# Two-port rules in the list scheduler of a fused attention and FFT-mixing MLP kernel, its weight conversion moved between engines, and spare buffers for the first chunks

## Chip, cores and metric

One NeuronCore of a Trainium2 chip runs the whole kernel. The metric is device time in microseconds (us) of one execution; the table below gives three runs of the kernel before and one execution recorded by the hardware profiler.

## The reference, cut to what matters

Eight batches of 8 heads, 576 positions and head dimension 64 pass a landmark (Nyström) attention with 32 landmarks and six Newton steps; its output goes through a two-dimensional FFT, a layer norm and an MLP of width 2048. Everything is float32.

```python
q_lm = q.reshape(B, H, 32, 18, D).mean(axis=3); k_lm = ...
A, Bm, C = sm(q, k_lm), sm(q_lm, k_lm), sm(q_lm, k)
Z = Bm.T / (norm1(Bm) * norminf(Bm) + 1e-6)
for _ in range(6): Z = 2 * Z - Z @ Bm @ Z
x = (A @ Z @ C @ v) as (batch, 576, 512)
u = x + real(fft2(x))
un = (u - mean(u)) / sqrt(var(u) + 1e-6)
return u + relu(un @ w_ch1) @ w_ch2
```

## The kernel before

A float32 product is made of three float16 matmuls: each operand is split into a high half and a low half (`mm3`). **Attention** of a batch (`attention`, `landmarks`, `mix`, lines 598 to 957) is a long chain of small steps that goes to and fro between TensorE and VectorE; it ends in `norm` (line 959), which writes normalized tiles of 128 rows and has them transposed by SyncE's DMA queue into `unT`. Batch 0 gives tiles 0 to 3, batch 1 tiles 4 to 8, batch 2 from tile 9 on. **Chunks** are pairs of tiles: 18 of them go through the MLP. Chunks 0 to 4 (`chunk`, line 998) make 8 hidden blocks each: 24 matmuls into a PSUM bank `hp`, a ReLU and a split into an SBUF tile, 12 matmuls into `acc`. Chunks 5 to 17 (`seven`, line 1065) do the second product with seven half products in place of eight, for which sums of blocks of the second weight are made once (`sums_of` and `block`, lines 1036 to 1063, 24 blocks that go to DRAM and back) and differences in place.

**Weights** (`weights`, line 521). Both weights arrive as 64-bit words in 16 tiles each (`w0`, the first weight, and `w1`, the second; profiles call both `w`). A tile takes: a shift of the low word, on GpSimd for all 32 tiles (table `XP`, line 89); two VectorE operations that put sign and exponent in; one ScalarE operation; a Gram matmul that finds a power-of-two scale; a scaling into the buffer `ws`, on ScalarE for the first weight and on VectorE for the second; a ScalarE copy that makes the high half; and a subtraction that makes the low half, on GpSimd for all 16 tiles of the first weight and for 8 of the second, on VectorE for the other 8 (table `LP`).

**Order.** No instruction is placed by hand. Every operation is recorded with an estimated cost (`cost_of`), a phase and a rank. `solve` (line 226) then simulates the engines with a list scheduler and emits each engine's queue in the order found. Attention of batch b has phase 100·b, weights 40 to 70, chunk work and sums 1000 and -1. Buffers come from pools with fixed counts (`SLOTS`, line 85); pools in `IN_ORDER` hand out their slots strictly in the order of the program. On the chip nothing but semaphores between producers and consumers holds the queues to the simulated times. All operations are issued from one line, so profile rows read L1149 and are told apart by tile names.

Of the kernel before, what the change touches and what calls it, by code (L numbers as in the profile page):

```python
# [11 lines left out]
F16 = mybir.dt.float16  # L12
# [74 lines left out]
LINK, PATIENCE = 0.05, 0.0  # L87
SEVEN, RING, LATE = 5, 10, 2
XP, LP = ((1, 1, 1, 1), (1, 1, 1, 1)), ((1, 1, 1, 1), (1, 0, 1, 0))

# [77 lines left out]
class Op:  # L168
    __slots__ = ("engine", "calls", "held", "took", "phase", "group", "margin", "seq", "before", "after", "tiles", "claims", "rank", "start", "end", "nbytes", "waits", "name")


class Order:


    def __init__(self):
        self.ops, self.phase, self.group, self.margin, self.bundle, self.claims = [], 0, 0, 0.0, None, []

# [8 lines left out]

    def op(self, engine, held, took, writes, reads, call, nbytes=0):
        o = self.bundle if engine == "PE" and self.bundle else None
        if o is None:
            o = Op()  # L190
            o.engine, o.calls, o.held, o.took, o.seq = engine, [], 0.0, 0.0, len(self.ops)
            o.phase, o.group, o.margin, o.nbytes = self.phase, self.group, self.margin, nbytes
            o.before, o.after, o.tiles, o.claims, o.name = {}, [], {}, self.claims, ""
# [32 lines left out]
    def solve(self):  # L226
# [10 lines left out]
        free = dict.fromkeys(engines, 0.0)  # L237
        pipe, now, done = 0.0, 0.0, []
        self.done = done
# [26 lines left out]
        while events:  # L266
            now = events[0][0]
            while events and events[0][0] <= now + 1e-9:
                _, _, what, o = heapq.heappop(events)
                if what == "ready":  # L270
                    soon[o.engine].pop(o, None)
                    heapq.heappush(ready[o.engine], ((o.phase, -o.rank if o.group >= 0 else 0.0, o.seq), o))
                elif what == "end":
                    for t in o.tiles:
                        if not t.pool.kept:
                            t.left -= 1
                            if not t.left:
                                t.pool.free.append(t.slot)
            for e in engines:
                if free[e] > now + 1e-9 or not ready[e]:  # L280
                    continue
                found = min((x for x in ready[e] if fits(x[1])), default=None, key=lambda x: x[0])
                if found is None or any(
# [17 lines left out]
                push(free[e], "free", o)  # L301
                push(o.end, "end", o)
# [12 lines left out]
class Engine:  # L315
# [5 lines left out]
    def __getattr__(self, name):  # L321
        def emit(out, *args, **kw):
            seen = [x for x in (*args, *kw.values()) if isinstance(x, View)]
            writes = [out] + ([kw["accum_out"]] if "accum_out" in kw else [])
            reads = [x for x in seen if x is not kw.get("accum_out")]
            held, took = self.cost(name, out, reads, (*args, *kw.items()))
            self.order.op(self.name, held, took, writes, reads, (self.engine, name, (out, *args), kw))
            self.order.ops[-1].name = name

        return emit  # L330


def cost_of(engine):
# [3 lines left out]
    def cost(name, out, reads, rest):  # L337
        n = max(width(v) for v in (out, *reads))
        pointers = sum(width(v) == 1 and width(out) > 1 for v in reads)
        psum = any(v.at_psum() for v in (out, *reads))  # L340
        if engine == "DVE":
            rate = 1.04e-3
            if name in ("tensor_scalar", "tensor_copy") and not psum:
                rate = 0.82e-3 if out.dtype == I32 else 0.6e-3
            elif out.dtype == I32:
                rate = 1.45e-3 if any(v.ap.ap[-1][0] > 1 for v in reads) else 1.2e-3
            elif name == "tensor_tensor" and not psum:
                rate = 1.4e-3
            if name == "reciprocal":
                rate = 6e-3  # L350
            return 0.07 + rate * n + 0.06 * pointers, 0.08
        if engine == "ACT":
            extra = 0.1 if any(isinstance(x, tuple) and x[0] == "accum_out" for x in rest) else 0.0
            return 0.09 + 0.79e-3 * n + (0.12 if pointers else 0.0) + extra, 0.1
        if name == "memset":
            return 0.1 + 1e-3 * n, 0.1
        power = 0.6 if any(x is ALU.pow for x in rest) else 0.0
        return 0.15 + (1.5e-3 if name == "tensor_scalar" else 2.1e-3) * n + power, 0.05

# [3 lines left out]
class Kernel:  # L363
# [157 lines left out]
    def weights(self):  # L521
# [437 lines left out]
    def norm(self, b, uts):  # L959
# [23 lines left out]
        for j, ut in enumerate(uts):  # L983
# [14 lines left out]
    def chunk(self, ch):  # L998
# [126 lines left out]
    def run(self):  # L1125
# [3 lines left out]
        for b in range(self.NB):  # L1129
            self.attention(b)  # L1130
            if b == 0:
                self.weights()
            while TCH * (chunks + 1) <= self.ntile:
                (self.seven if chunks >= SEVEN else self.chunk)(chunks)
                chunks += 1
                if chunks == SEVEN - 1:
                    for i in range(NF // 2):
                        self.sums_of(i)
                elif chunks == SEVEN:
                    for i in range(NF // 2):  # L1140
                        self.differences_of(i)
# [75 lines left out]
```

## Time and profile before

| what | us |
|---|---|
| runs of the kernel before | 1063.86, 1070.26, 1071.0 (median 1070.26) |
| the profiled execution, its own time | 1063.53 |
| span of that execution, first to last instruction | 1061.7 |
| TensorE busy in the span | 963.6 |
| VectorE busy | 780.1 |
| ScalarE busy | 466.3 |
| GpSimd busy | 420.5 |

The time of the profiled execution is 1.8 us more than its span. Busy times are unions over the span, so an engine's idle time is the span less its busy time. PE is TensorE's matmul stream, DVE VectorE, ACT ScalarE, POOL GpSimd, SPq SyncE's queue of DMAs.

### The profile page before, as it was taken

Reading aid. Unit: us, or ns where it says so; the run is one execution under the profiler, and the core shown is the slowest. Engines: PE = TensorE matmul, PEld = TensorE weight load, DVE = VectorE, ACT = ScalarE, POOL = GpSimd, SP = SyncE. Lnnn points to the kernel's source line nnn. Section 1 sums busy time; section 2 is a strip of 40 time slices with the busy share of each in tenths; the row PEclk is TensorE's granted clock in tenths of the full one; section 3 lists DMA queues with packets and bytes.
Section 4 is the critical chain, followed back from the end, with each engine's and each line's share of the span. In section 5 each row is a group of like instructions: output and inputs, shape, how many; then the busy total and the mean of one; then the engine's idle time right before and its main releaser. Section 6 shows DMA issues by size and latency. Waiting matters only on the chain.

```text
span 1061.7 us, 24997 instructions
## 1 busy us (share of the span) xinstructions
PE 963.6 (91%) x9858; PEld 758.3 (71%) x9858; DVE 780.1 (73%) x2015; ACT 466.3 (44%) x997; POOL 420.5 (40%) x383
## 2 busy tenths in 40 slices
PE   4565788989899999998999899998999999999997
PEld 3344645656576666886878787787878878888886
DVE  6998888997886865648877898587977646564343
ACT  4567453443453433434443554344543343343332
POOL 2358455357432145425133514343334422332332
PEclk9576879989999999999999999999999999999999
DMA  9565402414433310245333443335334312334331
GB/s 343 183 218 165 135 1 57 162 41 88 170 95 119 70 34 1 77 114 170 101 105 77 139 142 104 89 108 161 115 89 119 116 60 71 117 105 105 114 92 49
DMA packets 139398, 117.29 MB, mean 110 GB/s; under 512 B 66704, under 2 KB 128144, under 8 KB 139152
## 3 DMA queue, kind: packets, MB, share of 16 engines
q1 hardware_dynamic: 139280, 115.69, 36.1%
q8 instruction: 77, 1.26, 0.5%
q14 instruction: 41, 0.34, 0.1%
HBM read 88.91 MB, written 12.58 MB: 96 GB/s over the span
## 4 chain that ended last, share of the span: by engine, by line
PE 39%; DVE 28%; issue 15%; POOL 8%; ACT 5%; DMA 4%; SPq 1%; POOLq 0%; DVEq 0%; ACTq 0%
PE hp L1149 15%; PE at L1149 14%; PE acc L1149 10%; DVE sum L1149 5%; POOL h L1149 5%; DVE u L1149 3%; DVE w L1149 3%; DVE row L1149 2%; DVE mt L1149 2%; DVE h L1149 1%; DVE ws L1149 1%; ACT h L1149 1%; SPq L1149 1%; DVE Wx L1149 1%; ACT ws L1149 1%
## 5 line engine op out<-in xcount | busy, mean ns | idle before, releaser
L1149 PE MATMUL hp<-unT,w 128*128 128x256 f16 x3456 | 408.3, 274 | 1.4 <-ACT ws L1149 1.4
L1149 PEld LDWEIGHTS <-w 128*128 128x128 f16 (+1 forms) x3584 | 346.9, 99 | 74.0 <-DVE w L1149 20.7
L1149 PEld LDWEIGHTS <-h 128*128 128x128 f16 x2616 | 248.7, 98 | 85.0 <-issue 9.2
L1149 POOL TENSOR_TENSOR h<-sum,h 128x640 f16<-128x640 f32 x104 | 148.7, 1432 | 329.3 <-ACT h L1149 304.1
L1149 PE MATMUL acc<-w,h 128*128 128x256 f16 (+1 forms) x1680 | 270.0, 300 | 5.7 <-DVE h L1149 2.4
L1149 DVE TENSOR_TENSOR sum<-ws 128x256 f32<-128x256 f32 (+1 forms) x312 | 141.9, 506 | 133.7 <-ACT ws L1149 126.9
L1149 ACT CAST h<-sum 128x640 f16<-128x640 f32 x104 | 75.4, 725 | 109.6 <-DVE sum L1149 108.4
L1149 PE MATMUL at<-big,h 128*128 128x256 f16 x936 | 123.0, 274 | 0.0
L1149 ACT ACTIVATE ws<-hp 128x512 f32<-128x512 f32 x104 | 61.9, 595 | 136.4 <-PE hp L1149 135.7
L1149 POOL TENSOR_TENSOR w<-ws,w 128x512 f16<-128x512 f32 (+1 forms) x40 | 45.1, 1142 | 37.6 <-ACT w L1149 36.0
L1149 POOL TENSOR_TENSOR row<-row,row 128x512 f16<-128x512 f32 x36 | 45.7, 1280 | 32.7 <-ACT row L1149 31.9
L1149 PEld LDWEIGHTS <-mt 128*128 128x128 f16 x432 | 38.9, 101 | 22.1 <-issue 14.3
L1149 PEld LDWEIGHTS <-big 128*128 128x128 f16 (+1 forms) x768 | 39.7, 103 | 15.0 <-issue 9.6
L1149 DVE TENSOR_REDUCE lm<-big 128x32 f32<-128x576 f32 (+1 forms) x48 | 44.3, 942 | 4.2 <-DMA big<-k_dram 3.3
L1149 DVE TENSOR_TENSOR h<-ws,h 128x256 f16<-128x256 f32 x104 | 47.2, 454 | 0.0
L1149 POOL TENSOR_TENSOR mt<-mt,asum 128x512 f32<-128x512 f32 x14 | 15.3, 1110 | 74.6 <-DVE asum L1149 54.2
L1149 POOL TENSOR_TENSOR ws<-ws 128x256 f16<-128x256 f32 (+1 forms) x44 | 33.8, 774 | 27.8 <-ACT ws L1149 26.6
L1149 DVE SCALAR_TENSOR_TENSOR u<-at,scw,row 128x128 f32<-128x128 f32 (+3 forms) x120 | 39.5, 386 | 5.2 <-PE at L1149 4.3
L1149 ACT CAST h<-ws 128x256 f16<-128x256 f32 x104 | 42.1, 405 | 2.6
L1149 DVE SCALAR_TENSOR_TENSOR u<-acc,winv,u 128x512 f32<-128x512 f32 (+1 forms) x62 | 37.5, 631 | 7.0 <-PE acc L1149 6.8
L1149 ACT CAST row<-row 128x512 f16<-128x512 f32 x36 | 21.7, 615 | 45.9 <-DVE row L1149 40.6
L1149 ACT ACTIVATE h<-hp 128x512 f16<-128x512 f32 x36 | 21.5, 596 | 37.6 <-PE hp L1149 37.4
(181 smaller groups left out, 1312.4 us busy)
## 6 DMA issues: line engine op xcount, KB each, us to landing
big<-sums SPq DMA_DIRECT2D x312, 128.0 KB, 2.1
w<-w_dram SPq DMA_DIRECT2D x22, 512.0 KB, 7.3
big<-v_dram SPq DMA_DIRECT2D x16, 640.0 KB, 4.4
big<-q_dram SPq DMA_DIRECT2D x16, 584.0 KB, 6.4
big<-k_dram SPq DMA_DIRECT2D x16, 576.0 KB, 5.9
out_dram<-u SPq DMA_DIRECT2D x36, 256.0 KB, 2.2
big<-w_dram SPq DMA_DIRECT2D x10, 512.0 KB, 9.5
sums<-ws SPq DMA_DIRECT2D x24, 128.0 KB, 1.7
```

The source lines that it names most:

```text
L1149: getattr(engine, name)(*map(real, args), **{k: real(x) for k, x in kw.items()})
```

## The change

The scheduler gets a flag `port` on operations: on VectorE for those with no PSUM operand that read two full SBUF operands, or are a plain copy or `tensor_scalar`, of over 4 elements; on GpSimd for all but memsets. While one flagged operation runs in the simulation (and 0.05 us after it), no other flagged one starts. Costs in `cost_of` are set anew. The shifts of all 32 weight tiles go to ScalarE, all low halves to VectorE, and every second scaling of the second weight from VectorE to ScalarE. The third `unT` comes out of the pool `big`, and every third hidden block of chunks 0 to 4 (but the first four blocks of chunk 0) out of `sum`. The sums of blocks get batch 1's last operation as a predecessor.

```diff
-XP, LP = ((1, 1, 1, 1), (1, 1, 1, 1)), ((1, 1, 1, 1), (1, 0, 1, 0))
+XP, LP = ((2, 2, 2, 2), (2, 2, 2, 2)), ((0, 0, 0, 0), (0, 0, 0, 0))
...
+            best = {}
             for e in engines:
-                if free[e] > now + 1e-9 or not ready[e]:
-                    continue
-                found = min((x for x in ready[e] if fits(x[1])), default=None, key=lambda x: x[0])
+                if free[e] <= now + 1e-9 and ready[e]:
+                    shut = port > now + 1e-9
+                    best[e] = min((x for x in ready[e] if not (shut and x[1].port) and fits(x[1])), default=None, key=lambda x: x[0])
+            both = [best.get(e) for e in ("DVE", "POOL")]
+            if all(x is not None and x[1].port for x in both):
+                e = ("DVE", "POOL")[both[0][0] < both[1][0]]
+                best[e] = min((x for x in ready[e] if not x[1].port and fits(x[1])), default=None, key=lambda x: x[0])
...
+                if o.port:
+                    port = free[e] + PORT
...
-            return 0.07 + rate * n + 0.06 * pointers, 0.08
+            full = sum(width(v) > 1 for v in reads)
+            quick = name in ("tensor_scalar", "tensor_copy") and not psum
+            rate = 6e-3 if name == "reciprocal" else 0.58e-3 if quick and out.dtype != F16 else 1.04e-3
+            return 0.07 + rate * n + 0.03 * pointers, 0.08, not psum and (full > 1 or quick) and n > 4
...
-                if XP[w][f % 4]:
+                if XP[w][f % 4] == 1:
                     self.G.tensor_scalar(x, low.bitcast(U32), 2.0**-29 - 2.0**-39, -0.4995, ALU.mult, ALU.add)
+                elif XP[w][f % 4] == 2:
+                    A.activation(x, low.bitcast(U32), AF.Copy, bias=-0.4995, scale=2.0**-29 - 2.0**-39)
...
-                    if w:
+                    if w and f2 % 2:
                         V.tensor_scalar(src, slots[w][f2], scale, None, ALU.mult)
...
-                self.unT.append(self.new("unT").bitcast(F16)...)
+                self.unT.append(self.new("big" if len(self.unT) == 2 else "unT")[:, 0:1024].bitcast(F16)...)
...
-            t = self.mid(512) if ch == 0 and i < 4 else self.new("h")[:, 0:512]
+            t = self.mid(512) if ch == 0 and i < 4 else self.new("sum" if i % 3 == 2 else "h")[:, 0:512]
...
+            if b == 1:
+                self.second = self.order.ops[-1]
...
+                    self.order.gate = (self.second,)
                     for i in range(NF // 2):
                         self.sums_of(i)
+                    self.order.gate = ()
```

GpSimd's queue near its start, before and then after; `w` rows with `TENSOR_SCALAR` are the shifts of raw weight words, `mt` and `row` belong to batch 0's attention and norm, `wp0r` to the scale of the first weight.

```order
L1149 MEMSET Wx 128x1024
L1149 TENSOR_SCALAR w_110<-w_111 128x512 x9
L1149 TENSOR_TENSOR mt_78<-mt_77 128x256
L1149 TENSOR_SCALAR w_110<-w_111 128x512
L1149 TENSOR_TENSOR mt_77<-mt_78,mt_77 128x512
L1149 TENSOR_TENSOR mt_75<-mt_78 128x256
L1149 TENSOR_TENSOR mt_78<-mt_75,mt_78 128x512
L1149 TENSOR_SCALAR w_110<-w_111 128x512 x3
```

```order
L1160 MEMSET Wx 128x1024
L1160 TENSOR_TENSOR mt_78<-mt_77 128x256
L1160 TENSOR_TENSOR mt_74<-mt_78,mt_74 128x512
L1160 TENSOR_TENSOR mt_75<-mt_78 128x256
L1160 TENSOR_TENSOR mt_78<-mt_75,mt_78 128x512
L1160 TENSOR_TENSOR r_188<-ve_186,mhalf 128x2
L1160 TENSOR_TENSOR r_189<-ve_187,mhalf 128x2
L1160 TENSOR_TENSOR wp0r_205<-wp0f_203,mhalf 128x1
```

The shifts have left this queue, and in it batch 0's norm (`r`) now comes straight behind its attention.

VectorE's queue where batch 0's tiles are normalized (`row<-u`), before and then after; `w_110<-ws` rows are low halves of the first weight, `wea` and `wsa` its scales.

```order
L1149 TENSOR_SCALAR row_79<-u_88,mv_185,r_193 128x512
L1149 TENSOR_SCALAR wp0r_206<-wp0r_206 128x1
L1149 TENSOR_SCALAR wp0f_203<-at_103 128x1
L1149 SCALAR_TENSOR_TENSOR w_110<-w_111,w_110 128x512
L1149 RECIPROCAL wea<-wp0r_206 128x1
L1149 TENSOR_SCALAR wsa<-wp0r_206 128x1
L1149 SCALAR_TENSOR_TENSOR w_110<-h_96,w_110 128x512
```

```order
L1160 TENSOR_SCALAR row_79<-u_88,mv_185,r_193 128x512
L1160 TENSOR_TENSOR w_110<-ws_97,w_110 128x512
L1160 TENSOR_TENSOR w_110<-ws_98,w_110 128x512
L1160 TENSOR_TENSOR w_110<-ws_99,w_110 128x512
L1160 TENSOR_TENSOR w_110<-ws_97,w_110 128x512
L1160 SCALAR_TENSOR_TENSOR w_110<-h_96,w_110 128x512
L1160 TENSOR_SCALAR wp0r_206<-wp0r_206 128x1
```

Four low halves now stand in VectorE's queue right behind the norm, each of which waits for a ScalarE copy.

SyncE's queue at the end of batch 1's attention, before and then after; `sums` are the sums of weight blocks, `k_dram` to `v_dram` the loads of batch 2, `unT_92` and `big_66` the transposed tiles of chunks 2 and 3.

```order
L1149 DMA sums_213<-ws_98 128x256
L1149 DMA sums_215<-ws_99 128x256
L1149 DMA big_66<-k_dram 128x1152
L1149 DMA big_70<-q_dram 128x1168
L1149 DMA big_63<-k_dram 128x1152
L1149 DMA big_64<-q_dram 128x1168
L1149 DMA sums_216<-ws_97 128x256
L1149 DMA sums_218<-ws_99 128x256
L1149 DMA sums_217<-ws_98 128x256
L1149 DMA big_67<-v_dram 128x5x256
L1149 DMA sums_220<-ws_99 128x256
L1149 DMA big_68<-v_dram 128x5x256
```

```order
L1160 DMA_TRANSPOSE big_66<-row_80 128x4x128
L1160 DMA_TRANSPOSE unT_92<-row_79 128x4x128
L1160 DMA_TRANSPOSE big_66<-row_80 128x4x128
L1160 DMA_TRANSPOSE unT_92<-row_79 128x4x128
L1160 DMA_TRANSPOSE big_66<-row_82 128x4x128 x2
L1160 DMA_TRANSPOSE unT_92<-row_84 128x4x128 x2
L1160 DMA_TRANSPOSE unT_93<-row_81 128x4x128 x2
L1160 DMA big_70<-k_dram 128x1152
L1160 DMA out_dram<-u_86 128x512
L1160 DMA big_63<-q_dram 128x1168
L1160 DMA big_64<-k_dram 128x1152
L1160 DMA big_69<-q_dram 128x1168
```

Before, batch 2's loads and the first sums stood ahead of the transposes that end batch 1; now both stand behind them.

## Rows read from the trace of the kernel before

**Rows 1.** The page's part 1: span, then busy us of each engine.
```profile
span 1061.7 us, 24997 instructions
...
PE 963.6 (91%) x9858; PEld 758.3 (71%) x9858; DVE 780.1 (73%) x2015; ACT 466.3 (44%) x997; POOL 420.5 (40%) x383
```

**Rows 2.** Busy time by stage: window, length, PE, PEld, DVE, ACT, POOL, clock, DMA share, GB/s.
```profile
0.00:25.00 25.00, 11.33 (x134) 7.16 (x135) 16.37 (x55) 12.34 (x27) 6.70 (x12) 1.00 0.95 341
25.00:95.00 70.00, 38.00 (x403) 27.35 (x403) 67.75 (x164) 43.87 (x95) 40.19 (x39) 0.62 0.59 188
95.00:160.00 65.00, 54.32 (x463) 38.13 (x461) 56.29 (x113) 35.20 (x68) 35.70 (x31) 0.83 0.28 94
160.00:275.00 115.00, 103.78 (x1125) 67.55 (x1125) 100.34 (x266) 51.21 (x131) 63.02 (x69) 0.97 0.35 101
275.00:475.00 200.00, 198.98 (x2020) 144.06 (x2019) 138.51 (x379) 79.82 (x181) 68.87 (x73) 1.00 0.26 75
475.00:900.00 425.00, 402.50 (x4310) 336.43 (x4308) 322.18 (x848) 189.99 (x403) 155.79 (x124) 1.00 0.37 111
900.00:1056.00 156.00, 154.48 (x1412) 137.58 (x1410) 76.19 (x192) 53.90 (x95) 50.23 (x37) 1.00 0.34 98
```

**Rows 3.** Groups on VectorE, weight tiles: count, busy us, mean ns, idle before.
```profile
L1149 DVE SCALAR_TENSOR_TENSOR w<-big,w 128x512 int32<-128x512 int32 x20 | 18.6, 952 | 0.5 <-POOL w L1149 0.5
...
L1149 DVE SCALAR_TENSOR_TENSOR w<-h,w 128x512 int32<-128x512 int32 x16 | 14.6, 910 | 0.0
...
L1149 DVE SCALAR_TENSOR_TENSOR w<-w,w 128x512 int32<-128x512 int32 x16 | 12.5, 790 | 0.0
...
L1149 DVE SCALAR_TENSOR_TENSOR w<-w 128x512 int32<-128x512 int32 x12 | 9.9, 841 | 0.2 <-POOL w L1149 0.2
...
L1149 DVE TENSOR_TENSOR w<-ws,w 128x512 f16<-128x512 f32 x8 | 8.9, 1125 | 0.1
...
L1149 DVE TENSOR_SCALAR ws<-w,wsb 128x512 f32<-128x512 f32 x16 | 8.7, 587 | 1.1 <-POOL w L1149 1.1
```

**Rows 4.** VectorE in order of time, 83 to 85 us: start, length.
```profile
83.97 0.69 DVE L1149 SCALAR_TENSOR_TENSOR w<-w,w 128x512 int32<-128x512 int32 x1
84.57 0.68 DVE L1149 SCALAR_TENSOR_TENSOR w<-big,w 128x512 int32<-128x512 int32 x1
```

**Rows 5.** Groups on GpSimd, weight tiles.
```profile
L1149 POOL TENSOR_TENSOR w<-ws,w 128x512 f16<-128x512 f32 x24 | 34.5, 1455 | 11.3 <-ACT w L1149 9.7 <-PE acc L1149 1.3
...
L1149 POOL TENSOR_SCALAR w<-w 128x512 int32<-128x512 uint32 x22 | 18.7, 848 | 34.3 <-DMA w<-w_dram 30.5 <-DVE w L1149 3.0
...
L1149 POOL TENSOR_SCALAR w<-big 128x512 int32<-128x512 uint32 x10 | 9.3, 927 | 5.0 <-DVE w L1149 3.0 <-ACT ws L1149 1.3
```

**Rows 6.** Groups on ScalarE, weight tiles.
```profile
L1149 ACT ACTIVATE ws<-w,wsa 128x512 f32<-128x512 f32 x16 | 11.2, 717 | 3.0 <-DVE wsa L1149 2.8 <-POOL w L1149 0.2
...
L1149 ACT ACTIVATE h<-w 128x512 f32<-128x512 f32 x16 | 10.5, 671 | 11.1 <-DVE w L1149 9.0 <-issue 1.5 <-ACT ml L1149 0.6
```

**Rows 7.** In order of time, the transposes for chunk 0 and its first matmuls.
```profile
80.21 10.81 SPq L1149 DMA_TRANSPOSE unT<-row  x8
...
93.54 0.84 PE L1149 MATMUL hp<-unT,w 128*128 128x256 f16 x3
```

**Rows 8.** Groups on VectorE from 160 to 275 us: sums, landmarks of batch 2.
```profile
L1149 DVE TENSOR_TENSOR ws<-w 128x512 f32<-128x512 f16 x11 | 9.7, 881 | 1.3 <-DMA sums<-ws 1.3
...
L1149 DVE TENSOR_TENSOR ws<-ws 128x256 f32<-128x256 f32 x11 | 7.4, 671 | 0.0
...
L1149 DVE TENSOR_REDUCE lm<-big 128x32 f32<-128x576 f32 x4 | 3.0, 747 | 0.0
...
L1149 DVE TENSOR_REDUCE lm<-big 128x64 f32<-128x1152 f32 x2 | 2.7, 1346 | 0.0
```

**Rows 9.** Groups of the chunks from 5 on, whole span.
```profile
L1149 POOL TENSOR_TENSOR h<-sum,h 128x640 f16<-128x640 f32 x104 | 148.7, 1432 | 329.3 <-ACT h L1149 304.1 <-PE at L1149 25.1
...
L1149 DVE TENSOR_TENSOR sum<-ws 128x256 f32<-128x256 f32 x208 | 115.0, 590 | 133.7 <-ACT ws L1149 126.9 <-POOL h L1149 3.9 <-ACT RE L1149 1.5
```

More of the change, by code (lines that the diff above doesn't have):

```diff
@@ L87 @@
 LINK, PATIENCE = 0.05, 0.0
-SEVEN, RING, LATE = 5, 10, 2
-XP, LP = ((1, 1, 1, 1), (1, 1, 1, 1)), ((1, 1, 1, 1), (1, 0, 1, 0))
+SEVEN, RING, LATE, PORT = 5, 10, 2, 0.05
+XP, LP = ((2, 2, 2, 2), (2, 2, 2, 2)), ((0, 0, 0, 0), (0, 0, 0, 0))
 class Tile:
@@ L168 @@
 class Op:
-    __slots__ = ("engine", "calls", "held", "took", "phase", "group", "margin", "seq", "before", "after", "tiles", "claims", "rank", "start", "end", "nbytes", "waits", "name")
+    __slots__ = ("engine", "calls", "held", "took", "phase", "group", "margin", "seq", "before", "after", "tiles", "claims", "rank", "start", "end", "nbytes", "port", "name")
 class Order:
     def __init__(self):
-        self.ops, self.phase, self.group, self.margin, self.bundle, self.claims = [], 0, 0, 0.0, None, []
+        self.ops, self.phase, self.group, self.margin, self.bundle, self.claims, self.gate = [], 0, 0, 0.0, None, [], ()
     def claim(self, *views):
@@ L185, in claim, with op @@
             self.claims.append(t)
-    def op(self, engine, held, took, writes, reads, call, nbytes=0):
+    def op(self, engine, held, took, writes, reads, call, nbytes=0, port=False):
         o = self.bundle if engine == "PE" and self.bundle else None
@@ L191, in op @@
             o.engine, o.calls, o.held, o.took, o.seq = engine, [], 0.0, 0.0, len(self.ops)
-            o.phase, o.group, o.margin, o.nbytes = self.phase, self.group, self.margin, nbytes
-            o.before, o.after, o.tiles, o.claims, o.name = {}, [], {}, self.claims, ""
+            o.phase, o.group, o.margin, o.nbytes, o.port = self.phase, self.group, self.margin, nbytes, port
+            o.before, o.after, o.tiles, o.claims, o.name = dict.fromkeys(self.gate), [], {}, self.claims, ""
             self.claims = []
@@ L237, in solve @@
         free = dict.fromkeys(engines, 0.0)
-        pipe, now, done = 0.0, 0.0, []
+        pipe, port, now, done = 0.0, 0.0, 0.0, []
         self.done = done
@@ L278, in solve @@
                                 t.pool.free.append(t.slot)
+            best = {}
             for e in engines:
-                if free[e] > now + 1e-9 or not ready[e]:
-                    continue
-                found = min((x for x in ready[e] if fits(x[1])), default=None, key=lambda x: x[0])
+                if free[e] <= now + 1e-9 and ready[e]:
[5 more added lines that the diff above has]
+                best[e] = min((x for x in ready[e] if not x[1].port and fits(x[1])), default=None, key=lambda x: x[0])
+            for e in best:
+                found = best[e]
+                if found is not None and not fits(found[1]):
+                    found = min((x for x in ready[e] if not x[1].port and fits(x[1])), default=None, key=lambda x: x[0])
                 if found is None or any(
@@ L300, in solve @@
                 done.append(o)
-                push(free[e], "free", o)
+                push(port if o.port else free[e], "free", o)
                 push(o.end, "end", o)
@@ L325, in emit @@
             reads = [x for x in seen if x is not kw.get("accum_out")]
-            held, took = self.cost(name, out, reads, (*args, *kw.items()))
-            self.order.op(self.name, held, took, writes, reads, (self.engine, name, (out, *args), kw))
+            held, took, port = self.cost(name, out, reads, (*args, *kw.items()))
+            self.order.op(self.name, held, took, writes, reads, (self.engine, name, (out, *args), kw), port=port)
             self.order.ops[-1].name = name
@@ L341, in cost @@
         if engine == "DVE":
[L342 to L350, printed above, removed]
-            return 0.07 + rate * n + 0.06 * pointers, 0.08
+            full = sum(width(v) > 1 for v in reads)
+            quick = name in ("tensor_scalar", "tensor_copy") and not psum
+            rate = 6e-3 if name == "reciprocal" else 0.58e-3 if quick and out.dtype != F16 else 1.04e-3
+            return 0.07 + rate * n + 0.03 * pointers, 0.08, not psum and (full > 1 or quick) and n > 4
         if engine == "ACT":
             extra = 0.1 if any(isinstance(x, tuple) and x[0] == "accum_out" for x in rest) else 0.0
-            return 0.09 + 0.79e-3 * n + (0.12 if pointers else 0.0) + extra, 0.1
+            return 0.09 + 0.79e-3 * n + (0.06 if pointers else 0.0) + extra, 0.1, False
         if name == "memset":
-            return 0.1 + 1e-3 * n, 0.1
-        power = 0.6 if any(x is ALU.pow for x in rest) else 0.0
-        return 0.15 + (1.5e-3 if name == "tensor_scalar" else 2.1e-3) * n + power, 0.05
+            return 0.1 + 1e-3 * n, 0.1, False
+        power = 0.5 if any(x is ALU.pow for x in rest) else 0.0
+        return 0.14 + (1.15e-3 if name == "tensor_scalar" else 1.9e-3) * n + power, 0.05, True
     return cost
@@ L989, in norm @@
             if i % TCH == 0:
-                self.unT.append(self.new("unT").bitcast(F16).rearrange("p (y c t) -> p y c t", y=2, c=KT))
+                self.unT.append(self.new("big" if len(self.unT) == 2 else "unT")[:, 0:1024].bitcast(F16).rearrange("p (y c t) -> p y c t", y=2, c=KT))
             unT, at = self.unT[-1], P * (i % TCH)
```

## Prediction

> **What bounds the kernel now.** I read the page's busy times first [rows 1]: TensorE is busy for 963.6 of 1061.7 us, so 98 us of idle time are all that a better order can win without less matmul work, and the change takes no matmul away. The stage table [rows 2] then says where those 98 us lie. TensorE idles 13.7 us in the first 25 (loads), 32.0 from 25 to 95, 10.7 from 95 to 160, 11.2 from 160 to 275, only 1.0 from 275 to 475, 22.5 from 475 to 900 and 1.5 up to 1056; the rest is the end. So there are two places to win: before 275 us, and the long middle where attention and chunks share the engines.
>
> In the first place VectorE is the bound. From 25 to 95 us it is busy 67.75 of 70, from 160 to 275 us 100.34 of 115, while ScalarE stays at 43.87 of 70 and GpSimd at 40.19 of 70 [rows 2]. Part of this is not work but waiting. Two weight operations that follow each other start 0.60 us apart and last 0.69 and 0.68 [rows 4], yet the four groups of the same shape average 0.79 to 0.95 us, and the eight low halves 1.13 [rows 3]. GpSimd works on weight tiles beside them: 34.5 + 18.7 + 9.3 = 62.5 us of shifts and low halves [rows 5]. Their neighbours on VectorE are what gets longer. Between the two numbers of rows 4, 0.60 for one in a row and 0.69 for one alone, I take 0.64 us for an undisturbed operation of 512 elements with two SBUF inputs.
>
> **The change part by part.**
>
> *Shifts and low halves.* All 56 weight operations leave GpSimd. VectorE's gain: 64 operations take 18.6 + 14.6 + 12.5 + 9.9 = 55.6 us now and would take 64 x 0.64 = 41.0, a gain of 14.6; the 8 low halves it has take 8.9 and would take 5.1, a gain of 3.8; together 18.4. The groups of rows 3 are 73.2 of VectorE's 124.0 us from 25 to 160, and the other 50.8 us must be stretched too. I have no row that separates them: between nothing and the quarter that the first group lost (12.7 us) I take 5, low, because many of them read PSUM or hold a few elements. VectorE's cost: 24 more low halves x 0.64 = 15.4, less 8 scalings at 8.7 / 16 = 0.54, 4.3, is 11.1. What GpSimd keeps in this stretch is 40.19 + 35.70 - 62.5 = 13.4 us, under a fifth, so a fifth of the stretch stays: 4. GpSimd's low halves waited 9.7 us for ScalarE's copies, 0.4 each [rows 5]; VectorE's eight waited 0.1 in all [rows 3]. Twenty-four that now stand in VectorE's own queue, with the weight and attention steps queued behind each, cost 0 to 9.7; I take 3. Against this GpSimd's power operations of norm and scale no longer stand behind shifts, a short wait in the chain to chunk 0: -2, between 0 and -5. Sum: -18.4 - 5 + 11.1 + 4 + 3 - 2 = -7.3, call it -7.
>
> The shift on ScalarE does not occur in the trace. The nearest rows are ScalarE's 512-wide operation on the same raw words, 0.671, and GpSimd's shifts, 0.848 and 0.927 [rows 5, 6]. At 0.671, 32 of them and 8 scalings of 0.717 add 27.2 us to ScalarE's 43.87 + 35.20 = 79.1 of 135; at GpSimd's price it would be 33 to 35. ScalarE then stands at 106 to 114 of 135, VectorE by the sum above nearer 117. I take 0.67 and cost it at nothing on the path: VectorE's own queue covers it. If that cover goes, see the third rival.
>
> *Spare buffers.* Chunks 0 and 1 make hidden blocks before the second weight is ready; each waits in a buffer. Two more buffers let one more block be made in TensorE's idle time before 160 us: 24 matmuls at 154.48 / 1412 = 0.109 us [rows 2], -2.6. Their bounds are 0 and two blocks, -5.2. The third `unT` lets chunk 3's transposes leave before chunk 1 is through; its block matmuls stand behind chunk 2 in TensorE's queue anyway, so nothing is taken for it.
>
> *Batch 1's second half.* From 160 to 275 us VectorE does sums of blocks, 9.7 + 7.4 us, and landmark sums of batch 2, 3.0 + 2.7 [rows 8]. By the order, 7 of the 22 sums operations and all six landmark operations stood ahead of batch 1's norm; they are now behind it: about 7 / 22 of 17.1 plus 5.7, or 11 us less in front of chunk 2. TensorE still has chunk 0's and chunk 1's second products to do there and idles for 11.2 us only, so that is the upper bound; the lower is nothing. I take about half: -6.
>
> *Sums later.* The 24 sums then meet batches 2 and 3. VectorE is idle for 61.5 us from 275 to 475 and GpSimd for 131.1 [rows 2]; that room takes the 17.1 us, and chunk 5, the first to need sums, comes at its end. I take +2 (0 to +10) for ReLU splits that stand behind them. Batch 2's loads move behind ten more microseconds of transposes (eight took 10.81 [rows 7]), but chunks 2 and 3 lie before TensorE at that time, 8 x 24 x 0.109 = 21 us each for the first product alone, so this costs nothing.
>
> *The flag itself* changes no instruction, only the order; from 475 us on I take 0, between -22.5 (all idle time there) and +10. By the row, operations `sum<-ws` average 0.590 us beside GpSimd's 1.432 us ones [rows 9], and TensorE is nevertheless busy 154.48 of 156 us at the end.
>
> The Trainium skill's page "SBUF — State Buffer", section "Who interferes with whom", says that issue order decides who blocks, and that the second of the two waits for the whole first instruction. By that rule a simulated gap separates nothing on the chip unless the queues run as simulated, which speaks against a large gain from the flag; were the gap kept, the sum would be that of the first rival. Rows 4 against rows 3 agree that someone waits; no row shows who came first.
>
> Sum: -7 - 2.6 - 6 + 2 = -13.6 on the profiled execution's 1063.5 us, which is 1049.9. That execution is as fast as the fastest of the three runs and 0.6% below their median; I give 1050.
>
> **The rivals.**
>
> 1. *The separation holds on the chip* in the middle as well: VectorE's chains for the ReLU splits shorten and TensorE gets back two thirds of its 22.5 us. For it speaks that VectorE is the busiest helper there, 322.18 of 425 [rows 2]; against it, that no semaphore enforces the gap. 1049.9 - 15 = 1035.
>
> 2. *Given back.* TensorE's idle time before 275 us shrinks by the same 13.6, but batches 2 and 3, with all sums on top, deliver later, and the loss turns up between 275 and 475 us, where now 1.0 us is idle. For it: VectorE is at 100.34 of 115 just before. Time 1060 to 1068, say 1063.
>
> 3. *ScalarE becomes the bound* of the weight stage, a slower kernel. Each tile now goes ScalarE (shift), VectorE, ScalarE, VectorE, and later ScalarE twice and VectorE; each hop waits in order behind attention. If the two engines take turns rather than overlap, the stage loses ScalarE's 27.2 and VectorE's 11.1 us against 18.4 gained: 1063.5 + 19.9 = 1083. It decides once ScalarE is busy over nine tenths of the stretch from 25 to 160 us while VectorE falls below eight tenths. Against it: ScalarE waits 9.0 us for VectorE in one group now [rows 6], not the other way round.
>
> **How the numbers follow.** Forecast (1041 to 1061): 0.60. Rival 1: 0.13. Rival 2: 0.15. Rival 3: 0.12. The range 1031 to 1070 takes in the first two rivals and leaves out most of the third. Faster or slower by over 1%, about what a measurement of this kernel can tell, means under 1059.6 or over 1081.0 against the median. Faster: 0.13 and most of the forecast, 0.53, together 0.66. Same: the rest of the forecast, 0.07, rival 2, and a quarter of rival 3, 0.25. Slower: 0.09.
>
> **What would show it.** Right: in the weight stage the four groups of rows 3 average under 0.72 us, GpSimd's time from 25 to 160 us falls below 20, chunk 0's first matmul comes before 90 us where it was at 93.54 [rows 7], chunk 2's well before it did, and TensorE's idle time before 275 us falls from 67.6 to about 54. Wrong: ScalarE fuller than VectorE there; idle time of TensorE that comes back between 275 and 475 us; or a middle whose idle time falls far below 22.5 us.

## The result, and the profile after

The changed kernel takes 1037.08 us (median of 4 runs, 1034.45 to 1038.95) against 1067.26 us (4 runs), a ratio of 0.9715 with a 95% interval of 0.9665 to 0.9764. The prediction was 1050, range 1031 to 1070: the time lies inside the range, 13 us under the forecast, below the forecast's own range and close to the first rival's 1035. The profiled execution took 1035.55 us with a span of 1033.8, where before it was 1063.53 and 1061.7.

The page's busy times, to be held against [rows 1]:

```profile
PE 955.7 (92%) x9858; PEld 753.1 (73%) x9858; DVE 746.8 (72%) x2031; ACT 485.0 (47%) x1037; POOL 353.2 (34%) x327
```

TensorE's idle time fell from 98.1 to 78.1 us, and its busy time by 7.9 for the same 9858 matmuls, so some of them ran at a higher clock. The same stages as in [rows 2] (length, busy us and count of each engine, granted TensorE clock, DMA share, GB/s):

```profile
0.00:25.00 25.00, 11.84 (x151) 7.82 (x152) 16.36 (x59) 13.45 (x30) 2.07 (x8) 0.98 0.96 342
25.00:95.00 70.00, 42.73 (x464) 31.75 (x462) 60.62 (x163) 52.71 (x113) 13.23 (x13) 0.72 0.58 186
95.00:160.00 65.00, 52.16 (x457) 33.34 (x455) 59.07 (x144) 48.13 (x93) 1.93 (x2) 0.84 0.29 94
160.00:275.00 115.00, 112.06 (x1172) 74.42 (x1168) 82.78 (x227) 44.79 (x108) 47.03 (x53) 1.00 0.28 78
275.00:475.00 200.00, 195.52 (x2048) 144.49 (x2046) 153.08 (x429) 93.06 (x218) 94.01 (x98) 1.00 0.32 98
475.00:900.00 425.00, 415.87 (x4445) 349.87 (x4443) 311.86 (x862) 189.70 (x403) 155.90 (x127) 1.00 0.40 114
```

Idle time is a row's length less its first busy time. Up to 275 us it was 67.6 and is 56.2; from 275 to 475 it was 1.0 and is 4.5; from 475 to 900 it was 22.5 and is 9.1; after 900 it was 7.0 and is 8.3. So the span's 27.9 us are 11.4 less idle before 275, 3.5 given back behind it, 13.4 won in the middle, 1.3 lost at the end, and the 7.9 of busy time. Those 7.9 go with the clock: 0.62 became 0.72 from 25 to 95 us and 0.97 became 1.00 from 160 to 275, while from 475 to 900 both kernels are at 1.00. By the traces' clock records TensorE was busy at half clock for 50.5 us before 275 us and now is for 35.1; half of the difference, an estimated 7.7 us, is nearly all of the 7.9.

VectorE's and then ScalarE's weight groups from 25 to 160 us, against [rows 3] and [rows 6] (busy us, mean ns, idle before):

```profile
L1160 DVE TENSOR_TENSOR w<-ws,w 128x512 f16<-128x512 f32 x32 | 22.3, 728 | 2.2 <-ACT w L1160 1.9
L1160 DVE SCALAR_TENSOR_TENSOR w<-big,w 128x512 int32<-128x512 int32 x20 | 13.0, 684 | 0.0
L1160 DVE SCALAR_TENSOR_TENSOR w<-h,w 128x512 int32<-128x512 int32 x16 | 10.9, 683 | 0.1
L1160 DVE SCALAR_TENSOR_TENSOR w<-w,w 128x512 int32<-128x512 int32 x15 | 10.1, 683 | 0.0
L1160 DVE SCALAR_TENSOR_TENSOR w<-w 128x512 int32<-128x512 int32 x12 | 7.9, 684 | 0.1
...
L1160 ACT ACTIVATE w<-w 128x512 int32<-128x512 uint32 x20 | 13.2, 664 | 3.3 <-DVE w L1160 2.0 <-DMA w<-w_dram 1.2
L1160 ACT ACTIVATE w<-big 128x512 int32<-128x512 uint32 x10 | 6.4, 665 | 1.6 <-DVE w L1160 1.4 <-ACT row L1160 0.2
```

The four groups of one shape, at 0.95, 0.91, 0.79 and 0.84 us before, are all at 0.68, the length of the single operations of [rows 4] (0.69 and 0.68), and a low half fell from 1.13 to 0.73. A shift on ScalarE takes 0.665 us. Chunk 0's first matmul, at 93.54 in [rows 7], now starts at 80.69:

```profile
80.69 0.37 PE L1160 MATMUL hp<-unT,w 128*128 128x256 f16 x1 [9.39 <-DMA unT<-row]
```

### The profile page after: what moved, and what is told of

It reads as the page before. It is cut to its first block, busy times and chain, and to the rows that moved or that the text cites. A ratio compares the mean times of both kernels' runs of the same rounds, so it can differ in the third digit from the quotient of the medians.

```text
span 1033.8 us, 24962 instructions
## 1 busy us (share of the span) xinstructions
PE 955.7 (92%) x9858; PEld 753.1 (73%) x9858; DVE 746.8 (72%) x2031; ACT 485.0 (47%) x1037; POOL 353.2 (34%) x327
## 4 chain that ended last, share of the span: by engine, by line
PE 23%; issue 10%; DVE 9%; POOL 5%; ACT 3%; DMA 0%; POOLq 0%; DVEq 0%; ACTq 0%
PE hp L1160 10%; PE at L1160 8%; PE acc L1160 5%; POOL h L1160 4%; DVE sum L1160 2%; DVE u L1160 2%; ACT h L1160 1%; DVE big L1160 1%; DVE Wx L1160 1%; ACT Wx L1160 1%; POOL row L1160 0%; DVE asum L1160 0%; ACT ws L1160 0%; DVE bn L1160 0%; DVE row L1160 0%
## 5 line engine op out<-in xcount | busy, mean ns | idle before, releaser
L1160 PE MATMUL hp<-unT,w 128*128 128x256 f16 x3264 | 389.0, 274 | 11.8 <-DMA unT<-row 10.2
L1160 PEld LDWEIGHTS <-h 128*128 128x128 f16 x2508 | 239.6, 98 | 71.2 <-issue 6.6
L1160 POOL TENSOR_TENSOR h<-sum,h 128x640 f16<-128x640 f32 x104 | 152.1, 1464 | 300.6 <-ACT h L1160 291.2
L1160 PE MATMUL acc<-w,h 128*128 128x256 f16 (+1 forms) x1572 | 244.9, 295 | 3.0 <-ACT h L1160 1.1
L1160 DVE TENSOR_TENSOR sum<-ws 128x256 f32<-128x256 f32 (+1 forms) x312 | 134.8, 478 | 129.9 <-ACT ws L1160 118.8
L1160 PEld LDWEIGHTS <-mt 128*128 128x128 f16 x432 | 38.5, 100 | 15.2 <-issue 7.3
L1160 POOL TENSOR_TENSOR r<-ve,mhalf 128x2 f32<-128x2 f32 (+1 forms) x20 | 14.2, 710 | 86.6 <-DVE ve L1160 68.3
L1160 POOL TENSOR_TENSOR ws<-ws 128x256 f16<-128x256 f32 (+1 forms) x44 | 30.9, 709 | 35.7 <-ACT ws L1160 33.4
L1160 PE MATMUL at<-big,qbd 128*64 128x288 f32 x128 | 23.1, 490 | 12.4 <-DVE qbd L1160 12.4
```

What stands on the lines that cost most here:

```text
L1160: getattr(engine, name)(*map(real, args), **{k: real(x) for k, x in kw.items()})
```

## The experiments

All settings are of the changed kernel unless a line says otherwise. The scheduler plans the whole program anew for each, so a time holds the part that was changed and whatever else the new order does. The table therefore gives TensorE's idle time by stretch, worked out from the windows of one profiled execution as above, and its busy time in the whole of it.

| setting | median us | ratio to before, 95% | idle 0-275 | 275-475 | 475-900 | busy |
|---|---|---|---|---|---|---|
| before | 1067.3 | | 67.6 | 1.0 | 22.5 | 963.6 |
| changed | 1037.1 | 0.9665 to 0.9764 | 56.2 | 4.5 | 9.1 | 955.7 |
| 1 no exclusion | 1063.0 | 0.9942 to 0.9981 | 55.2 | 9.3 | 24.3 | 966.7 |
| 2 old weight operations | 1064.7 | 0.9962 to 1.0005 | 73.0 | 10.9 | 9.4 | 961.9 |
| 3 no spare buffers | 1062.4 | 0.9937 to 0.9984 | 56.7 | 23.2 | 9.2 | 965.0 |
| 4 no gate on the sums | 1046.3 | 0.9762 to 0.9841 | 59.1 | 3.5 | 11.1 | 963.4 |
| 5 gap 0.06 | 1043.3 | 0.9752 to 0.9816 | 57.6 | 10.6 | 8.6 | 960.0 |
| 6 exclusion early only | 1063.3 | 0.9952 to 0.9990 | 55.8 | 7.4 | 26.5 | 963.5 |
| 7 exclusion late only | 1049.2 | 0.9791 to 0.9864 | 56.3 | 8.0 | 11.5 | 964.5 |
| 8 exclusion and costs alone | 1066.0 | 0.9974 to 1.0011 | 71.7 | 7.1 | 10.0 | 968.4 |
| 9 longer prices, no exclusion | 1044.6 | 0.9754 to 0.9839 | 55.0 | 8.1 | 12.3 | 957.6 |
| 10 shifts alone | 1050.3 | 0.9810 to 0.9895 | 65.9 | 2.2 | 9.6 | 962.1 |
| 11 low halves alone | 1049.7 | 0.9792 to 0.9885 | 63.8 | 4.5 | 8.0 | 963.9 |
| 12 exclusion after the weights | 1036.5 | 0.9676 to 0.9757 | 57.0 | 4.5 | 9.7 | 953.5 |

The busy time of the same 9858 matmuls goes from 953.5 to 968.4 us, so a difference between two times is never idle time alone.

**1, no exclusion**

```diff
-            self.order.op(self.name, held, took, writes, reads, (self.engine, name, (out, *args), kw), port=port)
+            self.order.op(self.name, held, took, writes, reads, (self.engine, name, (out, *args), kw))
```

> Everything of the change but the exclusion: the scheduler no longer holds VectorE's two-port operations and GpSimd's apart; costs, weight operations, buffers and the gate on the sums stay. In the changed kernel chunk 5's first matmul came at 408.2 us (before 423.4, 15.2 earlier) and from there to chunk 17's it took 575.0 (before 587.1, 12.1 less). Theory A, the exclusion made the 12.1 of the middle: the stretch from chunk 5 to chunk 17 returns to 585 to 589, VectorE's 128x256 sum<-ws from 475 to 900 us average about 0.62 again instead of 0.53, and the time is 1046 to 1052. Rival B, the new costs, the buffers or plain luck of the order made it: the middle stays within 4 us of 575 and the time is 1033 to 1042.

The windows up to 275, to 475 and to 900 us:

```profile
0.00:275.00 275.00, 219.83 (x2214) 147.94 (x2215) 227.34 (x600) 160.63 (x349) 72.64 (x82) 0.87 0.43 137
275.00:475.00 200.00, 190.67 (x1966) 138.18 (x1966) 155.18 (x398) 83.97 (x197) 85.08 (x87) 0.99 0.30 88
475.00:900.00 425.00, 400.73 (x4264) 333.90 (x4262) 304.54 (x835) 186.77 (x397) 149.32 (x122) 0.99 0.39 109
```

The middle is back at 24.3 us idle: theory A has the place right and the sizes not. From chunk 5's first matmul to chunk 17's it takes 591.4 us (A: 585 to 589), the 256-wide sums average 0.597 us (A: about 0.62), and the time is past A's 1046 to 1052: between 275 and 475 us 4.8 more is lost, and TensorE is busy 966.7 us in the whole run instead of 955.7, at a clock of 0.99 instead of 1.00 in both of these stretches. Up to 275 us, however, nothing is lost (55.2 against 56.2). Without the exclusion the other parts keep their early gain of 12.4 us over the kernel before and lose it again: 8.3 between 275 and 475 us, 1.8 in the middle, 3.1 in busy time.

**2, old weight operations; 3, no spare buffers; 4, no gate**

```diff
-XP, LP = ((2, 2, 2, 2), (2, 2, 2, 2)), ((0, 0, 0, 0), (0, 0, 0, 0))
+XP, LP = ((1, 1, 1, 1), (1, 1, 1, 1)), ((1, 1, 1, 1), (1, 0, 1, 0))
-                    if w and f2 % 2:
+                    if w:
```

> The changed kernel with shifts, low halves and scalings on the engines of before. Theory A, the weight operations' move made most of the 15.2 us up to chunk 5, by taking GpSimd from beside VectorE: GpSimd is busy about 70 us from 25 to 160 us instead of 15.2, chunk 0's first matmul comes at 88 to 94 instead of 80.7, chunk 5's 7 to 15 later than 408.2, and the time is 1044 to 1052. Rival B, the exclusion alone does it and the move adds little: chunk 5 within 4 us of 408 and the time is 1036 to 1041. Rival C, with the exclusion GpSimd's shifts hold VectorE up in the order itself: chunk 5 later than 423 and the time is over 1055.

```diff
-self.new("big" if len(self.unT) == 2 else "unT")[:, 0:1024]
+self.new("unT")
-self.new("sum" if i % 3 == 2 else "h")[:, 0:512]
+self.new("h")[:, 0:512]
```

> The changed kernel without the third transposed tile in a big buffer and without every third hidden block in a sum buffer. Theory A (my sum): one hidden block less in idle time before the second weight, 2.6 us, time 1038 to 1042. Rival B, the buffers carry chunks 2 and 3, which came 23 and 37 us earlier: chunk 3's first matmul comes 10 or more later than 273.5 and the time is 1044 to 1052. Rival C, nothing: 1035 to 1038.

```diff
-                    self.order.gate = (self.second,)
+                    self.order.gate = ()
```

> The changed kernel without the gate that holds the 12 sums of the second weight behind batch 1's last operation. Theory A (my sum): batch 1's second half carries the sums again, chunk 2's first matmul comes 4 to 8 us later than 220.6, and the time is 1040 to 1045. Rival B, the sums find idle time of VectorE and GpSimd there: chunk 2 within 3 us of 220.6 and the time is 1034 to 1039. Rival C, the sums were missed later: chunk 5 comes earlier than 408.2 and the time is under 1033.

Setting 2's first window, beside the changed kernel's:

```profile
0.00:275.00 275.00, 202.00 (x1983) 135.58 (x1984) 208.15 (x535) 129.32 (x278) 103.88 (x115) 0.88 0.41 129
```

```profile
0.00:275.00 275.00, 218.79 (x2229) 147.34 (x2230) 218.82 (x591) 159.07 (x341) 64.25 (x76) 0.89 0.42 134
```

With the exclusion on, the move of the weight operations is worth 16.8 us of TensorE's busy time by 275 us (2229 matmuls instead of 1983). Chunk 0's first matmul nevertheless comes early with the old weight operations, where setting 1, which moves them but has no exclusion, is late (setting 2, then setting 1):

```profile
79.47 0.37 PE L1160 MATMUL hp<-unT,w 128*128 128x256 f16 x1 [9.54 <-DMA unT<-row]
```

```profile
92.32 1.91 PE L1160 MATMUL hp<-unT,w 128*128 128x256 f16 x8
```

So A's 88 to 94 falls; GpSimd is busy 57.7 us from 25 to 160, not 70, and the time is past A's range. The loss sits from 95 to 160 us, where TensorE waits 13.5 us for VectorE's weight tiles instead of 9.4. Chunk 5 starts at 426.8 and the time is 1064.7: both of rival C's signs. Its reason, GpSimd's shifts, is at most part of it, for with the shifts alone back on GpSimd (setting 11 below) the time is 1049.7.

In setting 3 the early stretch is untouched, and chunk 3 starts 14.5 us later (288.0) as B has it, but the time is past B's 1044 to 1052, and it is lost in one place: chunk 5 still starts at 405.5, ahead of the changed kernel's 408.2. TensorE's wait behind that and the windows around it:

```profile
PE hp L1160 <- ACT ws L1160: 14.4, 1, 14.4
```

```profile
420.00:430.00 10.00, 4.29 (x31) 2.41 (x27) 8.33 (x25) 4.93 (x13) 6.75 (x8) 0.56 0.15 27
430.00:440.00 10.00, 0.00 (x0) 0.00 (x0) 5.08 (x6) 1.42 (x4) 8.81 (x10) 0.50 0.00 0
440.00:450.00 10.00, 6.80 (x39) 5.12 (x39) 6.71 (x12) 5.09 (x11) 5.87 (x7) 0.57 0.01 2
```

Here chunk 4 is over and the sixteen differences of the second weight (`differences_of`), which go through VectorE, GpSimd and ScalarE, hold up chunk 5; GpSimd is busy 8.81 of 10 us there. In the changed kernel TensorE has matmuls of the next batch's attention between those of chunk 5 (0.6 us of wait); here they had run out by 429 us. The stall costs more than its idle time: around it the clock is granted at half, 1.2 of 2.4 GHz. The 11.1 us of busy time in these rows, at 0.56 and 0.57, would have been an estimated 4.8 shorter at full clock (4.29 x 0.44 + 6.80 x 0.43). The same wait lasted 0.6 us in the changed kernel, 5.4 in setting 2 and 5.9 in setting 5, which have the buffers; whether the buffers as such prevent it, or this order missed, stays open.

Without the gate chunk 2 starts 3.1 us later (223.7 against 220.6), between rival B's 3 and theory A's 4 to 8, and 2.9 us of idle time come back before 275 us. The time is 9.2 longer, a little over A's 1040 to 1045, and 7.7 of that is busy time.

**5, a number that means nothing; 6 and 7, the exclusion in one half; 8, the exclusion alone**

```diff
-SEVEN, RING, LATE, PORT = 5, 10, 2, 0.05
+SEVEN, RING, LATE, PORT = 5, 10, 2, 0.06
```

> The changed kernel with one number moved that means nothing by itself: the gap kept after a port operation is 0.06 instead of 0.05 us. So far each part taken away alone cost 9 to 28 us. Theory A, the parts act by what they do: time 1033 to 1042, TensorE idle 475 to 900 us 8 to 12 us. Rival L, every setting gives an order of its own, most of them lose a stall of 10 to 30 us somewhere before 475 us and the changed kernel's is a picked one: time 1045 to 1065, with the middle's idle time still 8 to 12 and the loss in one or two stalls before 475 us.

```diff
-nbytes, port
+nbytes, port and self.ports
...
+            self.order.ports = b < 3
             self.attention(b)
```

> The changed kernel with the exclusion only for operations written down for batches 0 to 2 and chunks 0 to 5; from batch 3 on the scheduler knows no port. Theory A, the exclusion acts where it is on: chunk 0's first matmul stays at 80 to 82 us, TensorE's idle time from 475 to 900 us goes back from 9.1 to 20 to 25 (22.5 before, 24.3 without any exclusion), time 1045 to 1052. Rival B, the middle follows from the early order and not from the flag: idle there 8 to 12, time 1034 to 1042. With a stall before 475 us (rival L) either comes out 10 to 28 us longer, and the windows tell which.

The same with `b >= 3`:

> The other half: the exclusion only for batches 3 on and chunks 6 on. Theory A: chunk 0's first matmul at 90 to 93 us as without exclusion (92.3) instead of 80.7, TensorE idle 8 to 12 us from 475 to 900, time 1043 to 1052. Rival B: chunk 0 at 80 to 82 because the weight operations' move alone does it, or the middle's idle time at 20 or more. Rival L's stall before 475 us may add 10 to 28 us.

Setting 8 is setting 2 with the edits of 3 and 4 as well:

> The kernel before with the exclusion and the new costs alone: shifts and low halves stay on GpSimd, no spare buffers, no gate. Theory A: GpSimd busy about 70 us from 25 to 160, TensorE idle 8 to 12 us from 475 to 900 (22.5 before), chunk 0's first matmul at 79 to 86 (as in the run with the old weight operations, 79.5), time 1045 to 1058. Rival B, without the other parts the middle falls back too: idle there over 18, time 1060 to 1070. Rival L: a stall before 475 us of over 15, time 1060 or more with the middle at 8 to 12.

The middle's row of 6 and then of 7:

```profile
475.00:900.00 425.00, 398.55 (x4248) 331.39 (x4246) 312.14 (x832) 185.50 (x394) 146.24 (x120) 0.99 0.39 108
```

```profile
475.00:900.00 425.00, 413.52 (x4408) 347.16 (x4406) 308.74 (x867) 189.29 (x403) 153.29 (x126) 0.99 0.41 114
```

A gap of 0.06 moves the time by 6.2 us, to 1043.3, between theory A's 1042 and rival L's 1045, and the idle time between 275 and 475 us by 6.1; that much of any single time can be the draw of an order. The middle's idle time is not drawn in the same way: in every setting that had the exclusion there it idles 8.0 to 11.5 us, in the three with neither it nor the prices of setting 9 (before, 1 and 6) 22.5 to 26.5. Ten settings are not ten draws, since some share most of their order there (2 and 3 start chunks 11 to 17 within 0.5 us of each other), but 5 and 11 pace the chunks in ways of their own. Setting 6 keeps chunk 0's early start (80.4) and loses the middle, as theory A says, but more of it (26.5, A: 20 to 25), and its 1063.3 is 11 past A's range without one long stall. Setting 7 answers as theory A says, chunk 0 at 91.7, the middle at 11.5, time 1049.2. Setting 8 gives the middle's gain too (10.0), with chunk 0 at 80.2, and still wins nothing (1066.0, A: 1045 to 1058; GpSimd 58.2 us from 25 to 160, A: about 70), because the early stretches lose 4.1 and 6.1 more than before and the busy time 4.8.

**9, longer prices instead of the exclusion** (on top of setting 1)

```diff
+            slow = 2e-3 if name == "tensor_tensor" and not psum and full > 1 and 128 <= n <= 256 else 1.04e-3
-            rate = 6e-3 if name == "reciprocal" else 0.58e-3 if quick and out.dtype != F16 else 1.04e-3
+            rate = 6e-3 if name == "reciprocal" else 0.58e-3 if quick and out.dtype != F16 else slow
```

> The kernel without the exclusion (1063.0) with one more change: the scheduler's price for VectorE's SBUF additions and subtractions of 128 to 256 elements is raised from 1.04 to 2.0 ns an element, so that a 128x256 sum stands in the plan at 0.58 us, what it took there on the chip (0.597), instead of 0.34. Nothing keeps the engines apart. Theory P, the exclusion helps from 475 to 900 us only because the plan then has VectorE's results at the time the chip has them, so that TensorE's queue holds other work ahead of them: idle time there falls from 24.3 to 9 to 14, time 1045 to 1056. Theory X, it is the alternation itself, of GpSimd's subtraction and VectorE's sums, that the plan leaves behind on the chip: idle stays at 19 to 26 and the time at 1058 to 1068. A stall before 475 us may add 5 to 20 to either; the window of the middle decides.

From 475 to 900 us, VectorE's sums and TensorE's waits for VectorE's `h` and `u` (total, times, longest), first of setting 1, then of setting 9:

```profile
L1160 DVE TENSOR_TENSOR sum<-ws 128x256 f32<-128x256 f32 x126 | 70.4, 597 | 54.7 <-ACT ws L1160 53.2 <-POOL h L1160 1.3
L1160 DVE TENSOR_TENSOR sum<-ws 128x128 f32<-128x128 f32 x63 | 21.0, 334 | 0.0
```

```profile
PE acc L1160 <- DVE h L1160: 6.3, 5, 2.2
PE at L1160 <- DVE u L1160: 3.9, 5, 1.3
```

```profile
L1161 DVE TENSOR_TENSOR sum<-ws 128x256 f32<-128x256 f32 x133 | 67.8, 548 | 44.0 <-ACT ws L1161 43.5
L1161 DVE TENSOR_TENSOR sum<-ws 128x128 f32<-128x128 f32 x66 | 28.4, 431 | 0.0
```

```profile
PE acc L1161 <- DVE h L1161: 0.3, 1, 0.3
PE at L1161 <- DVE u L1161: 0.3, 1, 0.3
```

and setting 9's window of that stretch:

```profile
475.00:900.00 425.00, 412.66 (x4426) 346.80 (x4424) 328.59 (x869) 193.73 (x408) 157.60 (x128) 1.00 0.40 114
```

Idle time comes out as theory P says, not X (the time, 1044.6, is just under P's range). A block has two 256-wide sums and one of 128: 2 x 597 + 334 = 1528 ns in setting 1, 2 x 548 + 431 = 1527 here. The stretching is the same and nothing is kept apart, yet idle time falls from 24.3 to 12.3, and the waits for VectorE's results, 10.2 us in these two lines, are 0.6. So longer prices are enough and the alternation is not needed; P's "only", that the exclusion has no other effect, is not shown by this. In the changed kernel the same three take 2 x 533 + 416 = 1482 in this stretch:

```profile
L1160 DVE TENSOR_TENSOR sum<-ws 128x256 f32<-128x256 f32 x136 | 68.0, 533 | 46.8 <-ACT ws L1160 39.7 <-POOL mt L1160 3.8 <-POOL h L1160 2.6
L1160 DVE TENSOR_TENSOR sum<-ws 128x128 f32<-128x128 f32 x68 | 28.3, 416 | 0.0
```

Over the whole run its 256-wide sums take 0.520 us, where [rows 9] have 0.590. Counted one by one in the traces from 475 to 900 us, 44 of 135 of these sums overlap a GpSimd instruction in the changed kernel, 40 of 126 in setting 1 and 46 of 133 in setting 9; one that overlaps none takes 0.42 us in all three.

Against the kernel before the picture is less simple. TensorE's waits of 0.2 us or more for `h` and `u`, and the two largest of the others, from 475 to 900 us, before and then after:

```profile
PE at L1149 <- DVE Wx L1149: 7.5, 3, 2.8
PE at L1149 <- ACT ml L1149: 4.7, 6, 1.1
PE acc L1149 <- DVE h L1149: 2.1, 3, 1.6
PE at L1149 <- DVE u L1149: 1.3, 4, 0.5
PE acc L1149 <- DVE u L1149: 0.7, 1, 0.7
```

```profile
PE at L1160 <- DVE Wx L1160: 5.4, 3, 2.2
PE at L1160 <- ACT ml L1160: 1.7, 4, 0.7
PE at L1160 <- DVE u L1160: 0.5, 1, 0.5
PE acc L1160 <- DVE h L1160: 0.2, 1, 0.2
```

The waits for `h` and `u` fall from 4.1 to 0.7 us, a quarter of the 13.4 that the middle gains. The rest is spread over steps of attention, and in one of them, `ml`, TensorE waits for ScalarE; no run shows why these are shorter.

**10 and 11, half of the weight move; 12, looking for a better one**

Setting 10 keeps the old `LP` and scalings, setting 11 the old `XP`; setting 12 is setting 7 with `b >= 1`.

> The changed kernel with only the shifts moved (to ScalarE); the 24 low halves stay on GpSimd and the 16 second scalings on VectorE. TensorE's busy time up to 275 us was 218.8 in the changed kernel and 202.0 with none of the weight operations moved. Theory A, it goes by GpSimd's time: the shifts are 28 of its 62.5 us, so 7 to 8 of the 16.8 come back, busy 208 to 212. Rival B, the low halves, last in each tile's chain and longest on GpSimd, are nearly all of it: busy 200 to 206. Rival C, the shifts are: 215 or more. The time follows by the same number, 1040 to 1060, more with a stall before 475 us.

> The other half: low halves on VectorE and eight scalings on ScalarE, the 32 shifts stay on GpSimd. Theory A by GpSimd's time (34.5 of 62.5 us): busy up to 275 us 209 to 213. Rival B of the run before: 215 or more. Rival C: 200 to 206, since VectorE has the low halves on top and still the shifts beside it.

> Looking for a better one: the exclusion on for everything but batch 0, the weight work and chunks 0 and 1, which did better without it from 95 to 160 us (TensorE busy 61.1 without, 52.2 with) and worse from 25 to 95 (40.0 against 42.7). If only the sums of those stretches count: 6 us more of TensorE's work by 160, the middle's idle time at 9 to 12, time 1029 to 1034. If, as with the other settings, the order that follows loses something else before 475 us: 1036 to 1050.

TensorE's busy time up to 275 us is 209.1 with the shifts moved and 211.2 with the low halves moved (275 less the table's idle time). With 202.0 for neither, that is 7.1 and 9.2, which add up to 218.3 against 218.8 for both: both in theory A's ranges, the gain goes by GpSimd's time. By matmuls it is less clear: 2047 and 2089 by 275 us against 1983 for neither and 2229 for both, so the halves bring 64 and 106 and both together 246; busy time also depends on the clock, 0.87 and 0.91 here against 0.88 and 0.89. The times, 1050.3 and 1049.7, are as A has them. Setting 12 ties with the changed kernel: chunk 0 starts 11 us later (91.7) and costs nothing. TensorE's busy time by 160 us is 2.9 us more, not 6, and 1036.5 is in the range for an order that loses something elsewhere. No setting beat the changed kernel.

## Why the prediction came out as it did

**The early stretches: right in size by luck.** Call the parts of the sum a to e in their order: shifts and low halves -7, spare buffers -2.6, batch 1's second half -6, later sums +2, the flag itself 0. Terms a to d came to -13.6. Measured up to 475 us: -11.4 + 3.5 = -7.9 us of idle time, little over half of it, and another -7.9 of busy time, together -15.8. The sum, like its first sentence on the "98 us of idle time" that are all an order can win, counted idle time only. The busy time that the better clock gave back had no term, though [rows 2] show 0.62 and 0.83 there. The mechanism of term a held: the stretched groups returned to 0.68 (0.64 had been taken), GpSimd from 25 to 160 us fell to 15.2 us (under 20), ScalarE's shift cost 0.665 where 0.67 was taken. One reading in it was wrong: 4 of the 22 `w<-w` shifts of [rows 5], 4.7 of 18.7 us, ran before 25 us, so by the rows GpSimd kept 18.1 us in that stretch and not 13.4. The size of term a alone is open. Its two halves are 7.1 and 9.2 us of TensorE's busy time in the order with the exclusion; without it all early parts together gave 12.4 (207.4 us of busy time before, 219.8 in setting 1), where terms a, b and c had promised 15.6.

**Chunk 0's start: right number, wrong reason.** "Before 90 us" came true at 80.7, but the exclusion did it: without it there, settings 1, 7, 9 and 12 have 90.5 to 92.3 with all weight operations moved; with it and nothing moved, settings 2 and 8 have 79.5 and 80.2. And it was no sign of the time (setting 12).

**Buffers, gate, later sums.** Term b (-2.6) is not in the early idle time (56.7 without, 56.2 with); what the buffers did lay behind 405 us. Term c (-6) was 2.9 us of idle time in setting 4, inside its bounds of 0 to -11.2. Term d (+2) stands against 3.5 us more idle time from 275 to 475; setting 4, without the gate, has 1.0 less there than the changed kernel, so the gate explains 1.0 of it and the rest is open.

**The step that failed is term e, "the flag itself", which I set to 0; it is worth 13 to 17 us from 475 to 900** (9.1 and 11.5 us idle with it in the changed kernel and setting 7, against 24.3 in setting 1 and 26.5 in setting 6). On the profiled execution the forecast missed by 1035.55 - 1049.9 = -14.4 us: -13.4 are this term, -7.9 the busy time, +5.7 the early idle time that was forecast and not won, +1.3 the end. The first rival named place and size ("two thirds of its 22.5 us"), and I gave it 0.13, because no semaphore enforces the gap. That reason is sound but does not lead to the conclusion.

The chip does not keep the engines apart: a third of the 256-wide sums overlap a GpSimd instruction with the exclusion and without it (44 of 135, 40 of 126), and three sums still take 1.48 us in the changed kernel against 1.53. The Trainium skill's page "SBUF — State Buffer", section "Who interferes with whom", says that issue order decides who blocks. By that rule a simulated gap separates nothing by itself, and these rows agree.

What I missed is that the plan has two uses. It orders the queue of VectorE, and it tells TensorE's queue when VectorE will be done. The plan of setting 1 counts 0.34 us for a sum that takes 0.60, so by this reading TensorE's queue has the dependent matmul too early and waits at its head. That longer prices alone bring the idle time down (setting 9) shows that the plan's times are enough; that the exclusion works by the same way, by making them late where the chip is late, is the reading that fits both and was not shown by a run of its own. The kernel before had a price between, 0.43, and waits for `h` and `u` between, 4.1 us against 10.2 and 0.6, but 22.5 us idle in all. So against the kernel before, most of the gain lies in other waits and its cause stays open. The change itself lowered that price to 0.34 together with adding the exclusion, and no run has one with the old costs. Setting 9 is one price in one order, so how long a price must be is open.

**The rivals.** Rival 1 had the right time and place, but its separation did not hold on the chip. Rival 2 happened in part: 3.5 us came back from 275 to 475, and 8.3 in setting 1. Rival 3 did not: ScalarE is at 52.71 and 48.13 us of the weight stage's two stretches, VectorE at 60.62 and 59.07.

## What to carry to other kernels

In a list scheduler, price an operation at what it takes beside its neighbours on the chip: here a price of 0.34 us for 0.60 went with many small waits of the engine that bounds the kernel, and 0.58 without them (one price, one order). An exclusion in the plan can pay even where the chip does not follow it. Judge one part of a replanned kernel by its stretch of the profile, not by the total: here a change of 0.01 us in a constant moved the total by 6 us, while the middle's idle time stayed at 8.0 to 11.5 us in every run with the exclusion there. Count the clock with the idle time: here the better clock was worth as much (7.9 us) as the idle time won up to 475 us.

## What the runs showed of the hardware that was not expected

A stall was paid again in slow matmuls around it, but in part only: in setting 3 idle time from 275 to 475 us grew by 18.7 us over the changed kernel, and the busy time around the stall, at a clock of 0.56 and 0.57, by an estimated 4.8. The busy time of the whole run is 9.3 longer (965.0 against 955.7); the rest lies elsewhere, such as from 475 to 900 us, at 0.99 against 1.00. And taking the long operations away from GpSimd removed the stretching of VectorE's four weight groups (0.683 and 0.684), whereas alternating the two in the plan took 46 ns off three sums in the changed kernel and at most 113 (setting 5, 2 x 509 + 397 = 1415 against 1528).
